# A top-k attention and MLP kernel on one core: TensorE's order written by hand, transposes in transpose mode, division on GpSimd, weights converted piece by piece

## The chip, the core and the metric

The kernel runs on one core of a Trainium2 chip. The metric is the device time of one execution in microseconds (us); the median of several executions counts. PE is TensorE, DVE VectorE, ACT ScalarE, POOL GpSimd, SP the engine whose queue issues the DMAs.

## The reference

```python
batch, n_heads, seq, head_dim = (8, 8, 576, 64)          # q, k, v
n_tokens, d_model, d_ff = (4608, 512, 2048)              # x, w_in, w_out
scores = scale * np.matmul(q, k.transpose(0, 1, 3, 2))
kth = np.partition(scores, -top_k, axis=-1)[..., -top_k:-top_k + 1]     # top_k = 32
scores = np.where(scores >= kth, scores, -1000000000.0)
scores = scores - np.max(scores, axis=-1, keepdims=True)
attn = np.exp(scores)
attn = attn / (np.sum(attn, axis=-1, keepdims=True) + 1e-09)
x = np.matmul(attn, v)                                    # then (B,H,S,D) -> (B*S, H*D)
h = x @ w_in
g = np.where(h >= 1, h, np.where(h <= -1, 0.0, (h + 1) ** 2 / 4.0))
out = g @ w_out
```

The weights arrive as 64-bit floats, two 32-bit words each, and the kernel turns them into 32-bit floats itself. All arithmetic is in 32-bit floats. A 32-bit matmul stands as two records of PE in the trace; a transpose in transpose mode as one.

## The kernel before

**Attention.** A row tile is 128 queries. A batch has 576 rows, so four whole tiles (t = 0 to 3) and 64 rows over; the leftover rows are done for two heads at a time (t = NT). One step is one tile for one pair of heads; there are 144 steps (`steps`, numbered m), four for each whole tile and two for each tail. A step has five stages, each a function. `scores` makes 128x576 scores per head in two halves of 288 columns (PSUM tiles `sp`, 64 contraction rows each) and ACT copies them to `s`. `top_k` finds the 32 largest of each row on DVE: four rounds of MAX8 and three of MATCH_REPLACE8, for each of the two heads (L192, L195). `weights` masks and exponentiates on ACT (L207, L209), adds up the sums `z`, takes 1/z on DVE (`z`, `rz`), and POOL writes `diag`, the identity times 1/z. `transpose_w` multiplies each 128-column block of the weights by `diag` (`pw`, L226), which transposes and divides at once, and does the last 64 columns apart (`pwt`, 64 output columns, L231). `values` multiplies the transposed weights by v (`po`) into `xT`.

**MLP.** It works on chunks of three row tiles (CT = 3, 384 columns). For each of 16 blocks f of the hidden width there are four matmuls over the contraction (`ph`, L277), then ACT makes `r` (L281), POOL squares it (L283), and DVE makes `g` (L284). For each tile, 16 matmuls over f then give `py` (L290), which ACT copies out to `y` and SP stores.

**Weight conversion.** There are 32 pieces of 128x512 (`weight_piece`): six DVE instructions and five POOL instructions each (L80 to L99), 16 pieces for `w_in` and then 16 for `w_out`. All are placed in the steps before the first chunk is ready; the first MLP matmul comes after the last piece.

**Order.** The loop over m issues `top_k(m)`, `scores(m+1)`, `weights(m-1)`, `transpose_w(m-2)`, half of this step's side work, `values(m-2)`, the other half. Side work is a generator (first the pieces, then one chunk's MLP at a time) that is advanced at an even rate. A scheduler of the tile framework then decides the order on each engine. PSUM has two banks for `sp` (tag `sc`), two for transposes (`tr`), two for `ph`, one each for `po` and `py`. All engines run their queues in order.

Of the kernel before, what the change touches and what calls it, by code (L numbers as in the profile page):

```python
# [1 line left out]

# [12 lines left out]
TOP_K = 32  # L15
# [4 lines left out]
def kernel(  # L20
# [26 lines left out]
    CT = 3  # L47
    CW = CT * P
    SCALE = float(D) ** -0.5
    FAR = 2.0 ** 80  # L50

# [12 lines left out]

    v_tails = []
    for i in range(2):
        v_tails.append(const.tile([P, H, D], F32, name=f"v_tail{i}"))
        nc.gpsimd.memset(v_tails[i], 0.0)
# [4 lines left out]
    def weight_piece(pool, dst, src):  # L73
# [9 lines left out]
        nc.vector.scalar_tensor_tensor(out=top, in0=lo, scalar=29, in1=top,  # L83
                                       op0=ALU.logical_shift_right, op1=ALU.bitwise_or)
# [15 lines left out]

    def weight_pieces(pool):
        for kk in range(NK):
            for c in range(0, DFF, WC):
                weight_piece(pool, w_in[:, kk, c:c + WC], moe_w_in[kk * P:(kk + 1) * P, c:c + WC])
                yield
        for f in range(NF):
            for c in range(0, DM, WC):
                weight_piece(pool, w_out[:, f, c:c + WC], moe_w_out[f * P:(f + 1) * P, c:c + WC])
                yield

# [5 lines left out]
    def load_values(b):  # L116
# [3 lines left out]
        for j in range(2):  # L120
            nc.sync.dma_start(out=v_tl[j * TL:(j + 1) * TL, j::2, :],
                              in_=v[b, j::2, SM:S, :].rearrange("h p d -> p h d"))
        return v_in, v_tl
# [10 lines left out]

    def keys_of(b):
# [5 lines left out]
        for hp in range(NHP):  # L141
# [3 lines left out]
            pt = ps.tile([P, NT, P], F32, name="pk", tag="tr", bufs=2)  # L145
            for c in range(NT):
                nc.tensor.transpose(pt[:, c, :], k_in[:, c].rearrange("p j d -> p (j d)"), ident)
            nc.scalar.copy(kT[:, hp, 0:SM], pt.rearrange("p c n -> p (c n)"))
            if hp == 0:
                pt = ps.tile([P, NHP, TL], F32, name="pkt", tag="tr", bufs=2)  # L150
# [3 lines left out]
                nc.scalar.copy(kT[:, :, SM:S], pt)  # L154
            yield dict(kT=kT, v=v_in, v_tl=v_tl)

    def queries_of(q_in, t):
        n = P if t < NT else TL
        qT = stage.tile([P, NHP, n], F32, name="qT" if t < NT else "qTt")
        pt = ps.tile([P, NHP, n], F32, name="pq", tag="tr", bufs=2)  # L160
# [258 lines left out]
```

## Time and profile before

| what | us |
|---|---|
| median of three runs | 2151.63 (2151.48 to 2151.65) |
| profiled execution, its own time | 2151.82 |
| its span, first to last instruction | 2150.0 |
| PE busy | 1923.7 (89%) |
| DVE busy | 1649.7 (77%) |
| ACT busy | 1008.3 (47%) |
| POOL busy | 527.1 (25%) |

The profile has four kinds of views used below. A table by stretches gives each engine's busy time between two moments. A timeline lists instructions in order of time, runs of the same kind merged. The chain that ended last follows the program back from its end, so each of its rows says how long the path stood on one thing. Groups by line give a mean time of one instruction. PE's matmuls overlap at their ends, so what a run of them costs is better read from one start to the next, as the chain has it, than from the mean of one.

### The profile page before, as it was taken

To read this page: it belongs to the slowest core of one execution; us is meant where nothing else is said; L and a number is where in the kernel's file an instruction comes from. 1 tells how busy PE (TensorE), PEld (TensorE's weight loads), DVE (VectorE), ACT (ScalarE), POOL (GpSimd) and SP (SyncE) were. 2 spreads that over 40 slices of the span, in tenths; PEclk is the share of its full clock that TensorE was granted. 3 is DMA by queue.
4 is the path that set the end of the run, shared out by engine and by line. 5 is a ranking of instruction groups with operands and counts; after the bars stand their busy time and mean duration, and the time that the engine had idled before them with its cause. 6 is when DMAs were issued, how large, how long until landed. Compare 5 with 4: busy or idle time off the path is not lost.

```text
span 2150.0 us, 29200 instructions
## 1 busy us (share of the span) xinstructions
PE 1923.7 (89%) x10560; PEld 1158.1 (54%) x10560; DVE 1649.7 (77%) x3568; ACT 1008.3 (47%) x2341; POOL 527.1 (25%) x809
## 2 busy tenths in 40 slices
PE   4333459999999999999999999999999999999999
PEld 2222336556556556556556556556556556555575
DVE  5888799978768779878768779878678779767530
ACT  3222245555445445545445446555445445454331
POOL 4889862102112112102112112102112112112021
PEclk9756779999999999999999999999999999999999
DMA  6222200100010000000010001000010000000000
GB/s 147 72 68 74 69 23 6 40 25 11 13 38 18 20 13 27 19 25 11 13 38 18 20 13 28 18 26 10 13 37 16 11 11 6 11 11 1 11 6 15
DMA packets 98193, 56.41 MB, mean 26 GB/s; under 512 B 81152, under 2 KB 89344, under 8 KB 98048
## 3 DMA queue, kind: packets, MB, share of 16 engines
q1 hardware_dynamic: 98048, 54.54, 9.3%
q8 instruction: 83, 1.36, 0.3%
q14 instruction: 62, 0.51, 0.1%
HBM read 45.09 MB, written 9.44 MB: 25 GB/s over the span
## 4 chain that ended last, share of the span: by engine, by line
PE 67%; DVE 19%; ACT 5%; POOL 5%; issue 3%; DMA 0%; SPq 0%; POOLq 0%; ACTq 0%; DVEq 0%
PE py L290 20%; PE ph L277 19%; PE pw L226 10%; PE sp L181 9%; DVE tops L192 8%; DVE rest L195 7%; PE po L247 5%; ACT s L183 2%; PE pwt L231 2%; POOL keep L94 1%; POOL low L98 1%; POOL low L97 1%; ACT s L207 1%; ACT s L209 1%; ACT r L281 1%
## 5 line engine op out<-in xcount | busy, mean ns | idle before, releaser
L192 DVE MAX8 tops<-rest 128x8 f32<-128x576 f32 x864 | 614.5, 748 | 0.1
L277 PE MATMUL ph<-xT,w_in 128*128 128x384 f32 (+2 forms) x1664 | 543.1, 472 | 2.3 <-DVE g L284 2.3
L290 PE MATMUL py<-w_out,g 128*128 128x512 f32 x1152 | 529.0, 603 | 0.0
L226 PE MATMUL pw<-diag,s 128*128 128x128 f32 x2304 | 345.3, 298 | 163.5 <-POOL diag L216 163.5
L226 PEld LDWEIGHTS pw<-diag,s 128*128 128x128 f32 x2304 | 296.9, 202 | 256.6 <-POOL diag L216 173.4
L195 DVE MATCH_REPLACE8 rest<-tops,rest 128x576 f32<-128x576 f32 x576 | 424.6, 743 | 0.0
L277 PEld LDWEIGHTS ph<-xT,w_in 128*128 128x128 f32 x1664 | 293.4, 190 | 183.9 <-issue 21.6
L207 ACT ACTIVATE s<-s,tops 128x576 f32<-128x576 f32 x288 | 217.1, 774 | 339.5 <-DVE tops L192 329.2
L290 PEld LDWEIGHTS py<-w_out,g 128*128 128x128 f32 x1152 | 208.0, 190 | 230.0 <-issue 224.4
L283 POOL TENSOR_TENSOR r<-r 128x384 f32<-128x384 f32 (+2 forms) x208 | 161.8, 778 | 638.1 <-ACT r L281 638.1
L192 DVE MAX8 tops<-s 128x8 f32<-128x576 f32 x288 | 208.0, 750 | 143.7 <-ACT s L183 143.5
L181 PE MATMUL sp<-kT,qT 64*128 64x288 f32 x1024 | 241.6, 464 | 39.3 <-ACT s L183 34.0
L183 ACT ACTIVATE s<-sp 128x288 f32<-128x288 f32 x576 | 210.7, 408 | 94.8 <-PE sp L181 89.5
L281 ACT ACTIVATE r<-ph,half 128x384 f32<-128x384 f32 (+2 forms) x208 | 115.2, 554 | 298.0 <-PE ph L277 297.6
L284 DVE SCALAR_TENSOR_TENSOR g<-ph,r 128x384 f32<-128x384 f32 (+2 forms) x208 | 109.2, 525 | 157.3 <-POOL r L283 156.0
L209 ACT ACTIVATE s<-s,nb 128x576 f32<-128x576 f32 x288 | 223.0, 775 | 1.5 <-POOL nb L204 0.4
L195 DVE MATCH_REPLACE8 rest<-tops,s 128x576 f32<-128x576 f32 x288 | 212.3, 743 | 0.0
L227 ACT COPY wT<-pw 128x512 f32<-128x512 f32 x288 | 167.2, 585 | 91.9 <-PE pw L226 90.8
L181 PEld LDWEIGHTS sp<-kT,qT 64*128 64x128 f32 x1024 | 115.7, 188 | 150.1 <-ACT s L183 79.8
L216 POOL TENSOR_SCALAR diag<-ident,rz 128x128 f32<-128x128 f32 x288 | 123.0, 440 | 288.2 <-PE pwt L231 134.0
L204 POOL TENSOR_TENSOR nb<-tops 128x2 f32<-128x2 f32 x144 | 29.9, 208 | 655.2 <-DVE tops L192 243.8
L247 PEld LDWEIGHTS po<-wT,v_in 128*64 128x64 f32 x2048 | 111.8, 138 | 71.5 <-issue 58.7
(55 smaller groups left out, 1180.3 us busy)
## 6 DMA issues: line engine op xcount, KB each, us to landing
q_in<-in_q_dram SPq DMA_DIRECT2D x32, 256.0 KB, 3.0
v_in<-in_v_dram SPq DMA_DIRECT2D x8, 1024.0 KB, 6.2
k_in<-in_k_dram SPq DMA_DIRECT2D x64, 128.0 KB, 2.8
raw<-in_moe_w_in_dram SPq DMA_DIRECT2D x16, 512.0 KB, 3.9
raw<-in_moe_w_out_dram SPq DMA_DIRECT2D x16, 512.0 KB, 3.6
out_dram<-y SPq DMA_DIRECT2D x32, 256.0 KB, 2.4
v_tail<-in_v_dram SPq DMA_DIRECT2D x16, 64.0 KB, 5.4
k_tl<-in_k_dram SPq DMA_DIRECT2D x8, 128.0 KB, 3.1
```

Source lines behind the costliest of these rows:

```text
L181: nc.tensor.matmul(o, qT[d, g, :], kT[d, g, keys], start=True, stop=True)
L183: nc.scalar.activation(s[:, i, keys], sp[i], AF.Copy, scale=SCALE)
L192: nc.vector.max(out=tops[:, i, r:r + 8], in_=src[:, i, :])
L195: nc.vector.match_replace(out=rest[:, i, :], in_to_replace=tops[:, i, r:r + 8], in_values=src[:, i, :], imm_value=LOWEST)
L207: nc.scalar.activation(s[:, i, :], s[:, i, :], AF.Prelu, bias=tops[:, i, TOP_K - 1:TOP_K], scale=-1.0, alpha=1.0 / FAR)
L209: nc.scalar.activation(s[:, i, :], s[:, i, :], AF.Exp, bias=nb[:, i:i + 1], scale=-FAR, accum_out=z[:, i:i + 1])
L226: nc.tensor.matmul(pt[:, c, :], w[:, i, c * P:(c + 1) * P], diag[:, i, :], start=True, stop=True)
L227: nc.scalar.copy(wT[:, i], pt)
L247: nc.tensor.matmul(po[j * D:(j + 1) * D], v_in[:, h, c, :] if c < NT else v_tl[:, h, :], wT[:, j, c, :] if c < NT else wTt, start=(c == 0) ...
L277: nc.tensor.matmul(ph, w_in[:, kk, f * P:(f + 1) * P], xT[:, kk, 0:cw], start=(kk == 0), stop=(kk == NK - 1))
L283: nc.gpsimd.tensor_tensor(out=r, in0=r, in1=r, op=ALU.mult)
L290: nc.tensor.matmul(py, gs[f][:, i * P:(i + 1) * P], w_out[:, f, :], start=(f == 0), stop=(f == NF - 1))
```

## The change

TensorE's order is now the order of the program text (`tc.manual_schedule` for PE alone); the other engines are still scheduled by the framework. Within a step the text has `values(m-2)`, `scores(m+1)`, MLP pieces, `transpose_w(m-1)`, the transposes of queries and keys, MLP pieces. Weights of step m are made in step m, not m+1.

- `transpose_w` uses transpose mode with the identity, nine blocks a step; the tails of both heads are one block of 128 columns. For that the scores of the second head are stored with the 64 tail columns first (`main`, `tail`, `pieces`), and a second copy of v's tails is loaded by four more DMAs a batch.
- The division is a POOL instruction on the 128x576 weights of each head, in place of `diag`.
- Mask and exponential have other constants and one more small POOL instruction (`nkth`).
- A weight piece has four DVE, two POOL and two ACT instructions. Three pieces are converted a step; `w_in` goes by column blocks, and MLP work may start as soon as its own pieces are there.
- MLP chunks have at most two tiles, the first two and the last two have one. The MLP is a list of pieces with a cost each, spread over the steps that are left.
- PSUM: four banks in one ring (tag `a`) for everything of attention, three for `ph`, one for `py`. `s` has three buffers in place of four.

```diff
-    CT = 3
+    CT = 2
...
+    PER_STEP = 3
...
-        nc.vector.scalar_tensor_tensor(out=top, in0=lo, scalar=29, in1=top,
-                                       op0=ALU.logical_shift_right, op1=ALU.bitwise_or)
 
         unit = pool.tile([P, WC], U32, name="unit")
         nc.vector.tensor_scalar(unit, top, 0xFF800000, None, ALU.bitwise_and)
-        rest = pool.tile([P, WC], U32, name="rest")
-        nc.vector.tensor_scalar(rest, lo, 0x1FFFFFFF, None, ALU.bitwise_and)
-
-        keep = pool.tile([P, WC], U32, name="keep")
-        nc.vector.tensor_scalar(keep, hi, 0x7FFFFFFF, None, ALU.bitwise_and)
-        keep = keep.bitcast(F32)
-        nc.gpsimd.tensor_scalar(keep, keep, 1.125 * 2.0 ** -15, None, ALU.is_ge)
         low = pool.tile([P, WC], F32, name="low")
-        nc.gpsimd.tensor_scalar(low, rest, 2.0 ** -26, 2.0 ** -26, ALU.mult, ALU.mult)
+        nc.scalar.activation(low, lo, AF.Copy, scale=2.0 ** -52)
         nc.gpsimd.tensor_tensor(out=low, in0=low, in1=unit.bitcast(F32), op=ALU.mult)
         nc.gpsimd.tensor_tensor(out=low, in0=low, in1=top.bitcast(F32), op=ALU.add)
-        nc.gpsimd.tensor_tensor(out=dst, in0=low, in1=keep, op=ALU.mult)
+
+        size = pool.tile([P, WC], F32, name="size")
+        nc.scalar.activation(size, hi.bitcast(F32), AF.Abs)
+        nc.vector.scalar_tensor_tensor(out=dst, in0=size, scalar=1.125 * 2.0 ** -15, in1=low,
+                                       op0=ALU.is_ge, op1=ALU.mult)
...
-        for kk in range(NK):
-            for c in range(0, DFF, WC):
+        for c in range(0, DFF, WC):
+            for kk in range(NK):
...
+        for hp in range(NHP):
+            g = hp % 2
+            nc.sync.dma_start(out=v_tl[1][g * TL:(g + 1) * TL, 2 * hp:2 * hp + 2, :],
+                              in_=v[b, 2 * hp:2 * hp + 2, SM:S, :].rearrange("h p d -> p h d"))
...
-        st["s"] = s = att.tile([P, 2, S], F32, name="s", bufs=4)
+        st["s"] = s = att.tile([P, 2, S], F32, name="s", bufs=3)
         for hf in range(2):
-            keys = slice(hf * SH, (hf + 1) * SH)
-            sp = [ps.tile([P, SH], F32, name="sp", tag="sc", bufs=2) for _ in range(2)]
...
+            sp = [ps.tile([P, SH], F32, name="sp", tag="a", bufs=4) for _ in range(2)]
+            c0, c1 = hf * SH, (hf + 1) * SH
             for i in range(2):
                 for j in ([i] if t < NT else [0, 1]):
                     d = slice(j * D, (j + 1) * D)
                     g = hp if t < NT else hp + i
                     o = sp[i] if t < NT else sp[i][j * TL:(j + 1) * TL]
-                    nc.tensor.matmul(o, qT[d, g, :], kT[d, g, keys], start=True, stop=True)
+                    for a0, a1, k0 in pieces(i, j, c0, c1):
+                        nc.tensor.matmul(o[:, a0 - c0:a1 - c0], qT[d, g, :], kT[d, g, k0:k0 + a1 - a0],
+                                         start=True, stop=True)
...
+    def mask(x, nkth):
+        nc.scalar.activation(x, x, AF.Prelu, bias=nkth, alpha=FAR)
+
     def weights(st):
         s, tops = st["s"], st["tops"]
+        nkth = att.tile([P, 2], F32, name="nkth")
+        nc.gpsimd.tensor_scalar(nkth, tops[:, :, TOP_K - 1], -1.0, 1.0, ALU.mult, ALU.mult)
         nb = att.tile([P, 2], F32, name="nb")
         nc.gpsimd.tensor_tensor(out=nb, in0=tops[:, :, TOP_K - 1], in1=tops[:, :, 0], op=ALU.subtract)
         z = att.tile([P, 2], F32, name="z")
         for i in range(2):
-            nc.scalar.activation(s[:, i, :], s[:, i, :], AF.Prelu, bias=tops[:, i, TOP_K - 1:TOP_K], scale=-1.0,
-                                 alpha=1.0 / FAR)
-            nc.scalar.activation(s[:, i, :], s[:, i, :], AF.Exp, bias=nb[:, i:i + 1], scale=-FAR,
-                                 accum_out=z[:, i:i + 1])
+            mask(s[:, i, :], nkth[:, i:i + 1])
+            nc.scalar.activation(s[:, i, :], s[:, i, :], AF.Exp, bias=nb[:, i:i + 1], accum_out=z[:, i:i + 1])
         rz = att.tile([P, 2], F32, name="rz")
         nc.vector.tensor_scalar(z, z, 1e-9, None, ALU.add)
         nc.vector.reciprocal(rz, z)
-        st["diag"] = diag = att.tile([P, 2, P], F32, name="diag")
         for i in range(2):
-            nc.gpsimd.tensor_scalar(diag[:, i, :], ident, rz[:, i:i + 1], 1.0, ALU.mult, ALU.mult)
+            nc.gpsimd.tensor_scalar(s[:, i, :], s[:, i, :], rz[:, i:i + 1], 1.0, ALU.mult, ALU.mult)
 
 
     def transpose_w(st):
-        t, w, diag = st["t"], st["s"], st["diag"]
+        w = st["s"]
         st["wT"] = wT = att.tile([P, 2, NT, P], F32, name="wT")
         st["wTt"] = wTt = att.tile([P, P], F32, name="wTt")
         for i in range(2):
-            pt = ps.tile([P, NT, P], F32, name="pw", tag="tr", bufs=2)
+            pt = ps.tile([P, NT, P], F32, name="pw", tag="a", bufs=4)
             for c in range(NT):
-                nc.tensor.matmul(pt[:, c, :], w[:, i, c * P:(c + 1) * P], diag[:, i, :], start=True, stop=True)
+                nc.tensor.transpose(pt[:, c, :], w[:, i, main(i)][:, c * P:(c + 1) * P], ident)
             nc.scalar.copy(wT[:, i], pt)
-        pt = ps.tile([P, P], F32, name="pwt", tag="po")
-        for i in range(2):
-            if t < NT:
-                nc.tensor.matmul(pt[i * TL:(i + 1) * TL], w[:, i, SM:S], diag[:, i, :], start=True, stop=True)
-            else:
-                for j in range(2):
-                    nc.tensor.matmul(pt[j * TL:(j + 1) * TL, i * TL:(i + 1) * TL], w[:, i, SM:S],
-                                     diag[:, i, j * TL:(j + 1) * TL], start=True, stop=True)
+        pt = ps.tile([P, P], F32, name="pwt", tag="a", bufs=4)
+        nc.tensor.transpose(pt, w.rearrange("p i n -> p (i n)")[:, SM:SM + P], ident)
...
+        got = []
+        for f in range(NF):
+            got.append((NK * len(tiles), NK * (f * P // WC + 1), partial(hidden, f)))
+        for i in range(len(tiles)):
+            for f in range(0, NF, 2):
+                got.append((2 * DM // P, n_pieces - NF + f + 2, partial(final, i, f, f + 2)))
+        return got
...
-            chunks += [a[0:3], a[3:4] + c[0:2], c[2:4] + [tl]]
+            chunks += ([a[0:1], a[1:2]] if b == 0 else [a[0:2]]) + [a[2:4], c[0:2], c[2:4], [tl]]
...
-            chunks += [a[0:3], a[3:4] + [tl] + c[0:1], c[1:3], c[3:4]]
+            chunks += [a[0:2], a[2:4], [tl], c[0:2], c[2:3], c[3:4]]
...
     def advance(amount):
-        nonlocal due
+        nonlocal spent, due
         due += amount
-        while due >= 1.0:
-            due -= 1.0
-            next(side, None)
-
+        while pending and pending[0][1] <= converted and due >= pending[0][0]:
+            cost, _, work = pending.popleft()
+            due -= cost
+            spent += cost
+            work()
+        due = min(due, 8.0)
+
+    order = tc.manual_schedule(engines={mybir.EngineType.PE})
+    order.__enter__()
...
     for m in range(n + 2):
+        if 2 <= m:
+            values(state[m - 2])
+            state[m - 2] = None
+            for ch in [c for c in range(len(chunks)) if ready[c] == m - 2]:
+                pending.extend(mlp(xTs[ch], chunks[ch], mlp_pool))
+        share = (total - spent) / (n + 2 - m)
         if m < n:
             top_k(state[m])
         if m + 1 < n:
             begin(m + 1)
+        if m < n:
+            weights(state[m])
+        convert(PER_STEP / 2)
+        advance(share / 2)
         if 1 <= m <= n:
-            weights(state[m - 1])
-        if 2 <= m:
-            transpose_w(state[m - 2])
-        advance(rate / 2)
+            transpose_w(state[m - 1])
+        queries(m + 2)
```

The order on three engines, in the middle of the program. On PE the place is some steps in which a chunk's hidden blocks are made. `sp` are scores, `pw` and `pwt` the transposes of the weights, `po` the values, `ph` and `py` the two MLP matmuls, `pq` and `pk` transposes of queries and keys. Before:

```order
L277 MATMUL ph<-xT,w_in 128x384 x4
L162 MATMUL pq<-ident,q_in 128x128 x4
L226 MATMUL pw<-diag,s 128x128 x4
L181 MATMUL sp<-kT,qT 128x288 x2
L226 MATMUL pw<-diag,s 128x128 x3
L181 MATMUL sp<-kT,qT 128x288 x2
L226 MATMUL pw<-diag,s 128x128
L231 MATMUL pwt<-diag,s 64x128 x2
L277 MATMUL ph<-xT,w_in 128x384 x4
L247 MATMUL po<-wT,v_in 64x128 x8
L247 MATMUL po<-wTt,v_tail_81 64x128 x2
L290 MATMUL py<-w_out,g 128x512 x4
```

PE after the change, again one step and a bit:

```order
L269 MATMUL po<-wT,v_in 64x128 x8
L269 MATMUL po<-wTt,v_tail_83 64x128 x2
L206 MATMUL sp<-kT,qT 128x288 x4
L300 MATMUL ph<-xT,w_in 128x256 x8
L254 MATMUL pw<-ident,s 128x128 x8
L257 MATMUL pwt<-ident,s 128x128
L300 MATMUL ph<-xT,w_in 128x256 x12
L269 MATMUL po<-wT,v_in 64x128 x8
L269 MATMUL po<-wTt,v_tail_83 64x128 x2
L206 MATMUL sp<-kT,qT 128x288 x4
```

Scores now follow the values without a full-width matmul between them and are no longer broken up; transposes stand next to MLP pieces. Counted over the whole order, PE goes from one of the three kinds (128x64 tiles: `po` and the old `pwt`; 64-row tiles: `sp`; full width: the rest) to another 1043 times before and 431 times after.

On DVE the place is the end of one `top_k` and the start of the next. Before:

```order
L195 MATCH_REPLACE rest<-tops,rest 128x576 x2
L192 MAX tops<-rest 128x8 x2
L212 TENSOR_SCALAR z<-z 128x2
L284 SCALAR_TENSOR_TENSOR g<-ph,r 128x384
L213 RECIPROCAL rz<-z 128x2
L192 MAX tops<-s 128x8 x2
L195 MATCH_REPLACE rest<-tops,s 128x576 x2
```

DVE after:

```order
L221 MATCH_REPLACE rest<-tops,rest 128x576 x2
L218 MAX tops<-rest 128x8 x2
L307 SCALAR_TENSOR_TENSOR g<-ph,r 128x256 x2
L218 MAX tops<-s 128x8 x2
L221 MATCH_REPLACE rest<-tops,s 128x576 x2
L241 TENSOR_SCALAR z<-z 128x2
L218 MAX tops<-rest 128x8
L242 RECIPROCAL rz<-z 128x2
L307 SCALAR_TENSOR_TENSOR g<-ph,r 128x256 x2
```

Before, the `z` behind a `top_k` was that of the step before; now it is that of the same step, a few instructions into the next `top_k`.

On POOL the place is the queue around the division. Before:

```order
L283 TENSOR_TENSOR r<-r 128x384 x2
L204 TENSOR_TENSOR nb<-tops 128x2
L216 TENSOR_SCALAR diag<-ident,rz 128x128 x2
L283 TENSOR_TENSOR r<-r 128x384 x2
L204 TENSOR_TENSOR nb<-tops 128x2
```

POOL after:

```order
L306 TENSOR_TENSOR r<-r 128x256 x2
L244 TENSOR_SCALAR s<-s,rz 128x576 x2
L306 TENSOR_TENSOR r<-r 128x256 x3
L233 TENSOR_SCALAR nkth<-tops 128x2
L235 TENSOR_TENSOR nb<-tops 128x2
L244 TENSOR_SCALAR s<-s,rz 128x576 x2
```

The two divisions of 576 columns stand where the two `diag` of 128 columns stood, with squares of `r` queued right behind them.

## Rows read from the trace of the kernel before

**Rows 1.** Table by stretches: us, busy time and count per engine, granted PE clock, DMA.
```profile
0.00:358.00 358.00, 168.04 (x962) 115.49 (x962) 291.43 (x601) 121.17 (x277) 256.92 (x230) 0.76 0.25 69
358.00:2150.00 1792.00, 1755.66 (x9600) 1042.64 (x9599) 1358.30 (x2968) 887.10 (x2064) 270.18 (x579) 1.00 0.07 18
```
**Rows 2.** Chain that ended last, around 1111 us: start, us it stood there, what.
```profile
1111.13 1.98 PE pw L226 x16
1113.12 0.37 PE pwt L231 x4
...
1116.26 1.24 PE po L247 x20
1117.50 2.78 PE ph L277 x8
1120.28 0.44 PE pq L162 x4
...
1121.61 0.69 PE sp L181 x4
...
1122.94 1.00 PE sp L181 x3
```
**Rows 3.** The same chain, a chunk of two tiles (256 columns).
```profile
2053.14 3.65 PE ph L277 x16
```
**Rows 4.** Timeline of DVE around one `top_k`: start, us, engine, line, operation.
```profile
1002.05 0.68 DVE L212 TENSOR_SCALAR z<-z 128x2 f32<-128x2 f32 x1
...
1004.15 1.42 DVE L192 MAX8 tops<-s 128x8 f32<-128x576 f32 x2 [0.78 <-ACT s L183]
...
1006.94 1.41 DVE L192 MAX8 tops<-rest 128x8 f32<-128x576 f32 x2
...
1013.73 1.41 DVE L192 MAX8 tops<-rest 128x8 f32<-128x576 f32 x2
1015.06 0.15 DVE L212 TENSOR_SCALAR z<-z 128x2 f32<-128x2 f32 x1
```
**Rows 5.** Groups by line: count, busy us, mean ns of one, idle before.
```profile
L81 DVE SCALAR_TENSOR_TENSOR top<-raw,top 128x512 uint32<-128x512 uint32 x32 | 29.5, 921 | 0.0
L98 POOL TENSOR_TENSOR low<-low,top 128x512 f32<-128x512 f32 x32 | 40.6, 1268 | 2.5
L94 POOL TENSOR_SCALAR keep<-keep 128x512 f32<-128x512 f32 x32 | 60.5, 1892 | 7.3 <-DVE keep L92 7.3
L96 POOL TENSOR_SCALAR low<-rest 128x512 f32<-128x512 uint32 x32 | 26.5, 827 | 17.8 <-DVE rest L89 16.2
L204 POOL TENSOR_TENSOR nb<-tops 128x2 f32<-128x2 f32 x144 | 29.9, 208 | 655.2 <-DVE tops L192 243.8 <-DVE z L212 223.3 <-DVE rz L213 87.1
L284 DVE SCALAR_TENSOR_TENSOR g<-ph,r 128x256 f32<-128x256 f32 x16 | 6.8, 423 | 23.6 <-POOL r L283 23.6
```
**Rows 6.** Timeline around 210 us, the stretch of the weight conversion.
```profile
208.84 1.44 ACT L207 ACTIVATE s<-s,tops 128x576 f32<-128x576 f32 x2 [13.47 <-DVE tops L192]
...
209.44 0.42 DVE L80 TENSOR_SCALAR top<-raw 128x512 uint32<-128x512 uint32 x1
...
210.11 2.28 POOL L216 TENSOR_SCALAR diag<-ident,rz 128x128 f32<-128x128 f32 x2 [0.20 <-DVE rz L213]
...
211.61 0.19 ACT L209 ACTIVATION_READ_ACCUMULATOR s<-s,nb 128x1 f32 x1
```
**Rows 7.** The chain at the start.
```profile
2.96 0.61 SPq L121
...
27.71 1.32 DVE tops L192 x2
```
**Rows 8.** The chain at the end.
```profile
2134.89 1.78 PE ph L277 x16
...
2138.43 7.74 PE py L290 x18
...
2146.24 0.59 ACT y L295
```

More of the change, by code (lines that the diff above doesn't have):

```diff
@@ L1 @@
+from collections import deque
 from contextlib import ExitStack
+from functools import partial
 import concourse.bass as bass
@@ L66 @@
     for i in range(2):
-        v_tails.append(const.tile([P, H, D], F32, name=f"v_tail{i}"))
-        nc.gpsimd.memset(v_tails[i], 0.0)
+        v_tails.append([const.tile([P, H, D], F32, name=f"v_tail{i}{x}") for x in range(2)])
+        for x in v_tails[i]:
+            nc.gpsimd.memset(x, 0.0)
     WC = 512
@@ L132, in load_queries, with main, tail, pieces @@
         return q_in
+    def main(i):
+        return slice(0, SM) if i == 0 else slice(TL, S)
+    def tail(i):
+        return slice(SM, S) if i == 0 else slice(0, TL)
+    def pieces(i, j, c0, c1):
+        if i == j:
+            return [(c0, c1, c0)]
+        cuts = [(0, TL, SM), (TL, S, 0)] if i else [(0, SM, TL), (SM, S, 0)]
+        return [(max(a, c0), min(b, c1), o + max(a, c0) - a) for a, b, o in cuts if max(a, c0) < min(b, c1)]
     def keys_of(b):
@@ L153, in keys_of @@
                                         ident[0:TL, 0:TL])
-                nc.scalar.copy(kT[:, :, SM:S], pt)
+                for j in range(2):
+                    d = slice(j * D, (j + 1) * D)
+                    nc.scalar.copy(kT[d, :, tail(j)], pt[d])
             yield dict(kT=kT, v=v_in, v_tl=v_tl)
@@ L273, in mlp, with hidden @@
         gs = []
-        for f in range(NF):
-            ph = ps.tile([P, CW], F32, name="ph", tag="ph", bufs=2)[:, 0:cw]
+        def hidden(f):
+            ph = ps.tile([P, CW], F32, name="ph", tag="ph", bufs=3)[:, 0:cw]
             for kk in range(NK):
@@ L318, with convert @@
     ready = [max(m for m in range(n) if steps[m][3] == ch) for ch in range(len(chunks))]
-    units = [NF + len(tiles) * (NF // 4) for tiles in chunks]
-    n_pieces = NK * DFF // WC + NF * DM // WC
-    cvt = tc.tile_pool(name="cvt", bufs=1)
-    cvt_pool = cvt.__enter__()
-    mlp_pool = None
-    side, left, rate, due = weight_pieces(cvt_pool), n_pieces, n_pieces / (ready[0] + 1), 0.0
+    mlp_pool = ctx.enter_context(tc.tile_pool(name="mlp", bufs=1))
+    pieces_left = weight_pieces(mlp_pool)
+    pending = deque()
+    total, spent = sum(len(tiles) for tiles in chunks) * (NK * NF + NF * DM // P), 0
+    converted, owed, due = 0, 0.0, 0.0
+    def convert(amount):
+        nonlocal converted, owed
+        owed += amount
+        while owed >= 1.0 and converted < n_pieces:
+            owed -= 1.0
+            converted += 1
+            next(pieces_left)
     def advance(amount):
-        nonlocal due
+        nonlocal spent, due
         due += amount
-        while due >= 1.0:
-            due -= 1.0
-            next(side, None)
+        while pending and pending[0][1] <= converted and due >= pending[0][0]:
[6 more added lines that the diff above has]
+    order.__enter__()
     keys, xTs = {}, {}
@@ L346, with queries @@
     state = []
+    def queries(m):
+        if m < n and steps[m][0:2] not in qTs:
+            r = steps[m][0:2]
+            qTs[r] = queries_of(q_ins[r], r[1])
+            fetch(rounds.index(r) + 2)
     def begin(m):
         b, t, hp, ch, col = steps[m]
-        if (b, t) not in qTs:
-            qTs[b, t] = queries_of(q_ins[b, t], t)
-            fetch(rounds.index((b, t)) + 2)
         if ch not in xTs:
```

64 lines of the change are left out of this document (29 added, 35 removed).

## The prediction

> **What bounds the kernel now.** I read the table by stretches first. The program has two parts [rows 1]. In the first 358 us the weights are converted: DVE is busy 291 us of them and POOL 257, PE only 168, at a granted clock of 0.76 on average. In the other 1792 us PE is busy 1755.66 us (98%) at full clock, DVE 1358 (76%), POOL 270 (15%). So POOL and DVE set the first part and PE the second. The chain says what PE's time goes into [rows 2]: one step's transposes take 1.98 us in 16 records and its tail block 0.37, values 1.24, scores 0.69 where both halves find a bank and 1.00 where one waits. Sixteen records at 0.11 make 1.78, so about 0.2 us of the 1.98 is the change from one kind of tile to another; the 3.65 us of sixteen hidden records of 256 columns [rows 3] hold the same 0.2, which leaves 0.216 for a record. An output record takes 7.74 / 18 = 0.43 [rows 8].
>
> DVE's own price of a step comes from its timeline [rows 4]. From 1004.15 to 1006.94 it does two MAX8 and two MATCH_REPLACE8, 2.79 us; from 1013.73 to 1015.06 the last two MAX8, 1.33. A `top_k` is three of the first and one of the second, 9.70 us. `z` and `rz`, two instructions of 0.15 and a little between, make it 10.05 a step, or 1447 us for 144 steps. That does not change, and it becomes the floor.
>
> **PE after the change.** A transpose in transpose mode is one record: four `pq` take 0.44 us [rows 2], 0.11 each. Nine are 0.98 in place of 1.98 + 0.37, which saves 1.37 us a step, 197 us in all. Scores with four banks take 2 x 0.69 in place of 0.69 + 1.00, 0.3 less. The changes of tile kind fall from 1043 to 431; 612 at 0.2 would be 122 us, part of which is in the two savings already. Without MLP a step is then values 1.24, scores 1.38, transposes 0.98, changes 0.1: 3.7 us. The MLP itself hardly gets cheaper: a hidden block of two tiles is 8 x 0.216 = 1.73, two output matmuls 4 x 0.43 = 1.72.
>
> The Trainium skill speaks against the transposes: "TensorE: Matmul & The Clock Gate", part 4 (PE-mode transpose), gives about 275 ns for one in a kernel. The rows above have 0.11 us, so I use that; by the page's figure nine would be 2.5 us, and my sum would grow as in the rival below.
>
> **DVE, POOL and ACT.** Steps get `g` in smaller pieces: 352 in place of 208, 0.42 us for 256 columns [rows 5], some 0.38 on average with those of 128. Division: no row shows it. Below, one-input POOL work on 512 columns takes 0.83 (L96), above, 1.89 (L94) [rows 5]; for 576 columns that is 0.93 to 2.1. I take 1.0, nearest to L96, which also multiplies by constants; two make 2 us a step, and POOL's total stays far below a step. It lies beside other work as long as the transposes of a step come one step later. What can show is contention: a `z` took 0.68 instead of 0.15 [rows 4], and two `diag` took 2.28 us while DVE converted weights [rows 6]. POOL will be busy some third of the time, so 0.53 us in a third of the steps is 25 us on DVE; it lies inside the range and not in the sum. The Trainium skill has a rule here that speaks against the change: "GPSIMD Engine Reference", 8. Key points, says that GpSimd shares its SBUF interfaces with VectorE, and that VectorE is about twice as fast at such work. The 0.68 us agrees with the sharing. If a `z` were held in every step, 0.53 x 144 = 76 us would be added; a division moved to DVE would lengthen the engine that is the floor, so I keep it on POOL in the sum.
>
> **The wait that is added.** `z` of a step now stands in the next `top_k`, usually behind two MAX8 and two MATCH_REPLACE8, 2.79 us. What it waits for is longer: one small POOL instruction of 0.21 [rows 5], then mask and exponential of both heads on ACT, 208.84 to 211.80, 2.96 us [rows 6], and the hops between, 3.4 in all. Behind `z` on DVE stands the rest of that `top_k`, for which the next mask on ACT and so the next transposes wait. I walked DVE's written order and counted what stands between the last MAX8 and `z` at these prices: in steps 13 to 142 the shortfall from 3.4 us adds up to 119 us. It costs only in the steps that DVE sets.
>
> **The sum.** Start to the first MAX8: 27.7 us [rows 7]. Four DMAs of v's tails go ahead of the keys on SP, 4 x 0.65 from the 0.61 of one [rows 7], but DVE then did conversion work before its first MAX8 that may move: 29.
>
> Steps 0 to 12, with 32 pieces: 13 x 10.05 = 131. A piece on DVE is two instructions of 0.42 [rows 6], one of 0.92 (L81 [rows 5]), and a last one that no row shows; between 0.42 and 0.92, taken as 0.75 because it reads two tensors: 2.5, or 80 in all. POOL's two instructions of 1.27 [rows 5] stand between the third and the last of them, and DVE's order has some 1.4 us of `top_k` there, so 1.1 is waited: 35. With 28 small `g`, 8: together 254 us. PE has slack there, as it had before at its lower clock [rows 1].
>
> Steps 13 to 142, walking both orders and taking the longer engine in each step: 14 steps without MLP are DVE's 10.05, 141 (PE has 3.7 us there, or 7.4 at 1.2 GHz, the lower of its two levels; the mean of 0.76 in the first part lies between them [rows 1]). In 33 steps with 116 `g` DVE is longer, 33 x 10.05 + 116 x 0.38 = 376. In 75 steps PE is longer, 908: 3.7 each and 8.4 of MLP, mostly five pieces of 1.73. In the last 8 steps the pieces pile up to 12 us, 125. That is 1550. To it come the waits for `z` in the 47 steps of DVE, 33, and the 2% that PE was not busy while it set the time before, 30. Against it stands that the queues run ahead of each other: `s` has three buffers and `ph` three banks. Summed over three steps at a time, the longer engine makes 37 less. 1576.
>
> The end: values, transposes and the MLP of one tile, 8 x 1.78 + 32 x 0.43 = 28 [rows 8], with 1.2 before it, and from the last `py` to the end of the span 2150.0 - 2146.24 = 3.8: 33.
>
> 29 + 254 + 1576 + 33 = 1892 us of span. The profiled execution was 1.8 longer than its span (2151.82 against 2150.0) and 0.2 above the median, so I forecast **1894 us**, 12% less.
>
> **Rivals.** (1) The two fixed orders even out fully and PE alone sets the steps, 1420 us for steps 13 to 142 and 2% more: 29 + 254 + 1450 + 33 + 2 = 1768; with DVE's sum and all its waits instead, 1410 + 119 = 1529, it is 1847. For it: PE ran at 98% before with a DVE that was 76% busy. Against: each engine now needs nearly the whole step, 10.9 and 10.8 us.
>
> (2) The small waits do not hide in each other: all of `z`, no evening out, 2% more. 1894 + 86 + 37 + 30 = 2047. For it: in order queues do add up waits; before 16 `g` of one form DVE stood 23.6 us for POOL, 1.5 each [rows 5], with time to spare then.
>
> (3) Slower: the squares of `r` are queued right behind the division on POOL. If DVE reaches a `g` before its square is through, it stands still for the division, which itself waits for `rz` on DVE. At 2.1 us a head that is 4.3 us in each of the 77 steps with hidden blocks, 331 us: 2225. It turns the sign from 3.3 us a step on. Against it: by the written orders a `g` stands some 3 us or more of DVE work later than its square can be ready, so PE would wait for a bank first.
>
> (4) The change does not do what it says, the transposes get no cheaper: at 0.275 us nine cost 1.5 more; in the 83 steps of PE that is 124, in the 33 others 0.7 each, 23: 2041.
>
> **Chances and range.** Forecast, both engines by turns, 1847 to 1940: 0.48. Rival 1, 1768 to 1847: 0.22. Rival 2, 1940 to 2060: 0.22. Rival 3: 0.05. Rival 4: 0.03. The range of 8 in 10 takes the forecast whole, rival 1 from 1790 up and rival 2 to 1990: 1790 to 1990. The division at its high end or the pieces at 0.42 or 0.92 move it by 10 to 30 and lie inside. Faster by over 0.2%, which is what a measurement of this kernel can tell from no change: 0.94; the same 0.01; slower 0.05.
>
> **What would show it.** In the new profile: `pw` near 0.11 us a record and nine a step; DVE busy above 85% after 250 us; its idle time mostly before `z` and before MAX8 on new scores, not before `g`; the conversion over by 285 us; PE below 95%. It is wrong if idle time before `g` passes 250 us, if the division takes over 2.5 us, or if the step in the middle is over 13 us or under 11.

## The result and the profile after

The changed kernel takes 2019.48 us (median of four runs, 2017.94 to 2021.12), beside 2151.56 for the kernel before: a ratio of 0.9387, 95% interval 0.937 to 0.9403. It is faster, as forecast, but by 6% and not by 12%: the forecast was 1894, and its range ended at 1990. The profiled execution took 2018.67 us, with a span of 2016.9.

Four views show where the time lies. First the page, with its busy line and the shares of the chain of waits by engine:

```profile
PE 1717.6 (85%) x10128; PEld 1175.6 (58%) x10128; DVE 1608.3 (80%) x3648; ACT 1075.0 (53%) x2589; POOL 537.6 (27%) x1003
...
DVE 53%; PE 19%; ACT 12%; POOL 10%; issue 6%; DMA 1%; SPq 0%; POOLq 0%; DVEq 0%; ACTq 0%
```

The table by stretches, cut at the first MAX8 of step 13 (278.5 us) and of step 143, the last (1956.3):

```profile
core 0: us, PE busy (x) PEld busy (x) DVE busy (x) ACT busy (x) POOL busy (x), PEclk, DMA share, GB/s
0.00:278.50 278.50, 130.90 (x756) 95.95 (x757) 206.06 (x440) 133.95 (x293) 126.06 (x153) 0.73 0.31 89
278.50:1956.30 1677.80, 1530.13 (x9037) 1040.61 (x9035) 1385.88 (x3162) 923.37 (x2253) 400.13 (x822) 0.96 0.07 19
1956.30:2016.90 60.60, 56.53 (x340) 39.08 (x338) 16.40 (x46) 17.65 (x45) 11.37 (x28) 0.99 0.03 9
```

The middle, steps 13 to 142, takes 12.9 us a step, with PE busy 91% of it and DVE 83%. Neither engine is full, where before PE was 98% busy [rows 1], so something ties them together. The waits of the changed kernel (engine, line and tile, what it waited for, us in total, times, longest) name it:

```profile
ACT s L228 <- POOL nkth L233: 315.2, 126, 7.3
...
DVE tops L218 <- ACT s L209: 202.7, 81, 7.4
...
DVE g L307 <- POOL r L306: 71.3, 92, 15.6
PE pw L254 <- POOL s L244: 64.1, 9, 13.8
PE sp L206 <- ACT xT L282: 57.6, 35, 5.1
...
DVE z L241 <- ACT s L239: 48.2, 17, 5.1
```

DVE stands still for 203 us before the first MAX8 of a step, for the copies of the scores, and PE for 58 us in the middle of the scores, for the copy of `xT`. The prediction had looked for DVE's idle time before `z` as well; that is only 48 us. One step shows how it happens, in the timeline of all engines (start, us, instruction, and in brackets the idle time ahead of it with what ended it); step 42's `top_k` ends here and step 43's begins:

```profile
632.27 1.41 DVE L218 MAX8 tops<-rest 128x8 f32<-128x576 f32 x2
...
633.47 0.39 PE L269 MATMUL po<-wTt,v_tail 128*64 128x128 f32 x4
...
633.79 1.23 PE L206 MATMUL sp<-kT,qT 64*128 64x288 f32 x6
633.85 0.19 POOL L233 TENSOR_SCALAR nkth<-tops 128x2 f32<-128x2 f32 x1 [5.36 <-DVE tops L218]
...
634.07 1.44 ACT L228 ACTIVATE s<-s,nkth 128x576 f32<-128x576 f32 x2 [4.15 <-POOL nkth L233]
635.42 0.24 ACT L282 COPY xT<-po 128x128 f32<-128x128 f32 x1
635.56 0.41 ACT L209 ACTIVATE s<-sp 128x288 f32<-128x288 f32 x1
...
635.71 0.75 PE L206 MATMUL sp<-kT,qT 64*128 64x288 f32 x2 [0.69 <-ACT xT L282]
...
636.62 1.00 ACT L209 ACTIVATE s<-sp 128x288 f32<-128x288 f32 x3
637.43 1.42 DVE L218 MAX8 tops<-s 128x8 f32<-128x576 f32 x2 [3.74 <-ACT s L209]
```

`po` is ready at 633.86, but ACT copies it to `xT` only at 635.42: in ACT's order both masks of step 42 stand ahead of it, they wait for `nkth`, and that waits for the end of `top_k`. `po` and the four score tiles are five tiles in a ring of four banks, so the last two score matmuls wait for that copy. They then take 0.75 us by themselves, where six before them took 1.23. Behind the masks stand the copies of the scores too, with an exponential among them. So `top_k`, `nkth`, masks, `xT`, last scores and copies run one after the other: 9.86 us of `top_k` from 623.82 to 633.68 and 3.74 of idle time, 13.6 us a step, for which PE's own work would be 12.3 (3.7 and ten output matmuls at 0.86).

### The profile page after: what moved, and what is told of

Read it like the earlier page. It is cut to its first block, busy times and chain, and to the rows that moved or that the text cites. A ratio compares the mean times of both kernels' runs of the same rounds, so it can differ in the third digit from the quotient of the medians.

```text
span 2016.9 us, 29329 instructions
## 1 busy us (share of the span) xinstructions
PE 1717.6 (85%) x10128; PEld 1175.6 (58%) x10128; DVE 1608.3 (80%) x3648; ACT 1075.0 (53%) x2589; POOL 537.6 (27%) x1003
## 4 chain that ended last, share of the span: by engine, by line
DVE 53%; PE 19%; ACT 12%; POOL 10%; issue 6%; DMA 1%; SPq 0%; POOLq 0%; DVEq 0%; ACTq 0%
DVE tops L218 27%; DVE rest L221 20%; PE py L315 9%; PE ph L300 4%; ACT s L228 4%; ACT s L239 3%; DVE g L307 3%; POOL s L244 3%; ACT s L209 2%; POOL r L306 2%; PE sp L206 2%; POOL low L93 2%; PE po L269 2%; POOL low L94 2%; PE pw L254 2%
## 5 line engine op out<-in xcount | busy, mean ns | idle before, releaser
L300 PE MATMUL ph<-xT,w_in 128*128 128x256 f32 (+1 forms) x2816 | 560.4, 355 | 72.0 <-DVE g L307 71.8
L300 PEld LDWEIGHTS ph<-xT,w_in 128*128 128x128 f32 x2816 | 466.2, 197 | 158.0 <-DVE g L307 87.9
L228 ACT ACTIVATE s<-s,nkth 128x576 f32<-128x576 f32 x288 | 214.4, 772 | 315.4 <-POOL nkth L233 315.2
L244 POOL TENSOR_SCALAR s<-s,rz 128x576 f32<-128x576 f32 x288 | 217.6, 768 | 382.0 <-DVE rz L242 243.1
L306 POOL TENSOR_TENSOR r<-r 128x256 f32<-128x256 f32 (+1 forms) x352 | 187.8, 540 | 423.6 <-ACT r L304 418.4
L206 PE MATMUL sp<-kT,qT 64*128 64x288 f32 x1024 | 196.8, 452 | 60.2 <-ACT xT L282 51.2
L304 ACT ACTIVATE r<-ph,half 128x256 f32<-128x256 f32 (+1 forms) x352 | 148.2, 433 | 172.8 <-PE ph L300 141.3
L254 PE MATMUL pw<-ident,s 128*128 128x128 f32 x1152 | 163.5, 288 | 68.8 <-POOL s L244 64.1
L254 PEld LDWEIGHTS pw<-ident,s 128*128 128x128 f32 x1152 | 142.9, 149 | 119.5 <-POOL s L244 72.6
L307 DVE SCALAR_TENSOR_TENSOR g<-ph,r 128x256 f32<-128x256 f32 (+1 forms) x352 | 128.6, 368 | 76.4 <-POOL r L306 71.3
```

The lines of the kernel that those rows point to most:

```text
L206: nc.tensor.matmul(o[:, a0 - c0:a1 - c0], qT[d, g, :], kT[d, g, k0:k0 + a1 - a0], start=True, stop=True)
L228: nc.scalar.activation(x, x, AF.Prelu, bias=nkth, alpha=FAR)
L244: nc.gpsimd.tensor_scalar(s[:, i, :], s[:, i, :], rz[:, i:i + 1], 1.0, ALU.mult, ALU.mult)
L254: nc.tensor.transpose(pt[:, c, :], w[:, i, main(i)][:, c * P:(c + 1) * P], ident)
L300: nc.tensor.matmul(ph, w_in[:, kk, f * P:(f + 1) * P], xT[:, kk, 0:cw], start=(kk == 0), stop=(kk == NK - 1))
L306: nc.gpsimd.tensor_tensor(out=r, in0=r, in1=r, op=ALU.mult)
```

## The experiments

Every change below is made to the changed kernel. Four theories were tried on the 125 us by which the span is over its forecast: (A) ACT's order, as just told; (B) lumps, that PE is simply full in steps with five pieces of the MLP, and DVE's wait only shows it; (C) the ring of banks alone; (D) the granted clock, 0.96 in the middle, which the forecast had named for the steps without MLP and priced at nothing.

**mask_after: one mask behind the scores' copies.**

```
-                nc.scalar.activation(s[:, i, c0:c1], sp[i], ...)
+                st["copied"] = nc.scalar.activation(s[:, i, c0:c1], sp[i], ...).ins
...
-            mask(s[:, i, :], nkth[:, i:i + 1])
+            with tc.issue_after(after["copied"]) if after and i == 0 else nullcontext():
+                mask(s[:, i, :], nkth[:, i:i + 1])
```

`after` is the state of the next step; the guard itself binds instructions on ACT alone. The rest of the scheduler's orders on ACT, DVE and POOL changes with it; PE's stays.

> Edit: on ACT the first mask of a step is ordered behind the last copy of the next step's scores; nothing else. Theory A (ACT's order: in steps with output matmuls the mask of the step stands ahead of the copies of xT and of the next scores, so DVE waits through top_k, mask, xT, last scores, copy, 13.6 us a step): DVE's idle time before MAX8 on new scores falls from 203 us to under 110, PE's wait for xT from 58 to under 20, time 1930 to 1975. Theory B (the planner's lumps: PE is full in those steps, and DVE's wait only shows it): DVE's idle time moves elsewhere, time 2000 to 2030. A later mask could also make z late; then idle time before z grows from 48 us by what is won, and the time stays.

Measured 2007.39 us, 12 less: within B's range, but not as a test of A. PE's wait for `xT` is still 55.8 us: only head 0 was held, and ACT now takes the mask of head 1 first. DVE's wait for scores did not fall but rose, while the one before `z` went from 48 to 9:

```profile
DVE tops L218 <- ACT s L209: 234.0, 86, 7.0
...
DVE z L242 <- ACT s L240: 8.9, 6, 3.3
```

Half a test; the next one holds both.

**masks_after: both masks** (`if after and i == 0` becomes `if after`).

> Edit: as mask_after, with the masks of both heads behind the last copy of the next scores; in mask_after ACT simply took the mask of the other head first (one mask still ran ahead of xT in most steps), so its 12 us are half a test. Theory A (ACT's order): PE's wait for xT falls from 58 us to under 20, steps with 20 output records from 13.6 us to about 12.3, time 1950 to 1990. Theory B (lumps alone): 1998 to 2025, the idle time only changes its place, most likely to z, whose masks come later.

Measured 1907.52 us (1905.91 to 1908.32), 112 less than the changed kernel and beyond what either theory gave. The same place in this kernel's timeline:

```profile
615.48 1.41 DVE L218 MAX8 tops<-rest 128x8 f32<-128x576 f32 x2
616.05 1.09 PE L270 MATMUL po<-wT,v_in 128*64 128x128 f32 x16
616.98 0.39 PE L270 MATMUL po<-wTt,v_tail 128*64 128x128 f32 x4
...
617.30 1.24 PE L206 MATMUL sp<-kT,qT 64*128 64x288 f32 x8
617.41 0.27 ACT L283 COPY xT<-po 128x128 f32<-128x128 f32 x1 [3.99 <-PE po L270]
618.08 1.32 ACT L209 ACTIVATE s<-sp 128x288 f32<-128x288 f32 x4 [0.40 <-PE sp L206]
...
619.20 1.42 DVE L218 MAX8 tops<-s 128x8 f32<-128x576 f32 x2 [2.31 <-ACT s L209]
619.26 1.46 ACT L228 ACTIVATE s<-s,nkth 128x576 f32<-128x576 f32 x2
```

`xT` is copied as soon as `po` is ready, the eight score matmuls run as one group of 1.24 us, and the masks come last. The step takes 12.2 us in place of 13.6, which is PE's own work. Its waits say the same, and so does its chain by engine:

```profile
DVE tops L218 <- ACT s L209: 134.3, 63, 6.7
...
PE sp L206 <- ACT xT L283: 9.3, 7, 2.2
...
DVE z L242 <- ACT s L240: 6.6, 5, 3.1
```

```profile
PE 62%; DVE 20%; ACT 8%; POOL 7%; issue 3%; DMA 1%; SPq 0%; POOLq 0%; ACTq 0%; DVEq 0%
```

PE's wait for `xT` falls from 58 us to 9, DVE waits a third less for scores, and PE holds 62% of the chain where it held 19%. DVE is busy for 1608 us in both kernels, so what it waits less is what the kernel gains: 68 us before MAX8 on new scores and 42 before `z`. What the masks' later place was feared to do, hold `z` back, does not show, and one reason lies on DVE. Counted over its order in steps 13 to 142, 13 `z` of the changed kernel stand ahead of the next step's first MAX8, and 40 us of the wait before `z` fall on these. In masks_after none does, and 104 of 130 stand behind six instructions of the next `top_k`. So the 68 us go with the copies that the masks no longer hold up. The 42 come with a `z` that the scheduler put later, and no run holds that apart.

**x_first: masks behind the copy of `xT` only.** The same guard, on the copy in `values` of the same pass of the loop:

```
+            ran["xT"] = nc.scalar.copy(xT[:, hp, col:col + P], po).ins
...
+            with tc.issue_after(ran["xT"]) if ran else nullcontext():
+                mask(s[:, i, :], nkth[:, i:i + 1])
```

> Edit: ACT's masks of a step are ordered behind the copy of xT only (which gives po's bank to the last pair of score matmuls), not behind the copies of the scores. If the link that costs is the bank (xT's copy late, last scores alone on PE), most of masks_after's 112 us come back: 1905 to 1940, and PE's wait for xT falls under 20 us. If it is the copies of the scores themselves that stand behind the masks, PE's wait goes and DVE's idle time before MAX8 on new scores stays: 1970 to 2015.

Measured 1975.8 us. Its waits:

```profile
DVE tops L218 <- ACT s L209: 215.0, 83, 6.7
...
DVE z L244 <- ACT s L242: 9.5, 5, 5.9
...
PE sp L206 <- ACT xT L285: 7.8, 5, 3.0
```

PE's wait falls from 58 to 8 us and 44 us come off; the other 68 of the 112 come only when the copies of the scores go ahead of the masks as well. DVE's wait for scores is not shorter than in the changed kernel (215 against 203); what it waits less is 39 us before `z`, which again no longer stands ahead of the first MAX8, and 13 before `g`. How much of the 44 us is the bank's is therefore not shown. So the larger link is the one that the prediction did not see at all: new scores that lie ready in a bank while ACT waits with a mask for the `top_k` that DVE is in.

**ring5: five banks for `a`, two for `ph`.**

```
-tag="a", bufs=4   -tag="ph", bufs=3
+tag="a", bufs=5   +tag="ph", bufs=2
```

> Edit: five PSUM banks for po, scores and transposes, two for the hidden blocks. Theory C (five tiles in four banks: po and four score tiles): PE's wait for xT falls from 58 us to under 10 and the four score tiles keep running two at a time: 40 to 60 us less, 1960 to 1980. Theory A: scores get done but their copies still stand behind the mask, so DVE's idle time before MAX8 on new scores stays above 150 us and under 25 us is won, 1995 to 2020; with only two banks for hidden blocks, PE may wait for g and lose 10 to 20 of it.

Each tile with one of the tags has the new number. Measured 2064.03 us, 45 slower, which neither theory had. PE no longer waits for `xT`, but the third bank of the hidden blocks was worth more:

```profile
PE ph L300 <- DVE g L307: 173.2, 101, 25.2
```

That was 71.8 us in the changed kernel. DVE's wait for scores stays, at 207 us, as A had it. A bank for C has to come from somewhere, and eight are all in use here. The run tells little on C itself; x_first does that without a bank.

**warm: idle transposes to hold the clock.**

```
+        if not pending and converted >= n_pieces:
+            pd = ps.tile([P, P], F32, name="warm", tag="ph", bufs=3)
+            for _ in range(16):
+                nc.tensor.transpose(pd, ident, ident)
         due = min(due, 8.0)
```

> Edit: in half steps where no MLP piece is pending, 16 idle transposes of the identity run on PE, their result unread. Theory D (the granted clock: 0.96 on average from 400 us on, half rate in stretches that follow PE's idle time, which makes some 30 to 40 us): granted clock 0.98 or more in the middle, 20 to 40 us less, 1980 to 2000. Theories A and B: within 8 us of 2019, since steps without MLP are set by DVE and the heavy steps by their content.

Measured 2057.96 us, 38 slower, which no theory had. From 303 to 349 us, two steps without MLP and the two behind them, the clock does rise; first the changed kernel, then this one:

```profile
303.00:349.00 46.00, 37.95 (x273) 29.46 (x272) 42.48 (x97) 28.48 (x69) 11.44 (x23) 0.89 0.08 20
```

```profile
303.00:349.00 46.00, 41.97 (x358) 34.70 (x356) 42.67 (x97) 27.43 (x67) 10.21 (x21) 1.00 0.08 20
```

But the first step without MLP grows from 9.79 to 12.79 us: PE comes late for the next scores, and DVE waits 2.9 us for them (234 us in all, 203 before). **masks_warm** puts the same lines into masks_after, to take that link away.

> Edit: masks_after with warm's 16 idle transposes in half steps where no MLP piece is pending. In warm they took PE's slack away just where ACT's order then made DVE wait. If that coupling was why it lost, and the granted clock is worth something, 1880 to 1903 here. If the idle transposes simply make PE late for the next scores, 1915 to 1945 again.

Measured 1919.2 us, 12 over masks_after, although the mean clock is 0.954 and not 0.938. PE's slack in those steps was worth more than what the clock gave back, if it gave anything: no run separates the two, and a clock held in some other way was not tried. D stays open.

**plan_even and taut: other shares of the MLP.** In plan_even a step's share is what is pending divided by the steps until the next chunk is ready. In taut it is the largest constant rate that never runs dry before a chunk comes:

```
-        share = (total - spent) / (n + 2 - m)
+        ends = [(sum(len(t) for x, t in enumerate(chunks) if ready[x] + 2 < e), e)
+                for e in [r + 2 for r in ready if r + 2 > m] + [n + 2]]
+        share = max(0, min((128 * tiles - spent) / (e - m) for tiles, e in ends if tiles))
```

> Edit: the MLP's share of a step is what is pending divided by the steps until the next chunk is ready, in place of what is left of the whole program. Theory B (lumps): steps without MLP and steps with five pieces both go, a middle step takes 11.3 to 12 us in place of 12.9, and the last step is left with one chunk in place of two: time 1850 to 1930. Theory A (ACT's order): steps with output matmuls still take 13 us or more, and the time is 1970 to 2015.

> Edit: the MLP's share of a step is the largest constant rate that never runs out of work before a chunk is ready, so that most steps get four pieces (6.9 us of PE beside 3.7) and neither empty steps nor lumps stay, which plan_even still had at three places (two steps of 31 us each). Theory B: a middle step of 11 to 11.8 us, time 1800 to 1870. Theory A would still find output steps at 13 us or more, time above 1900.

Measured 1968.18 and 1958.18 us, 51 and 61 less. plan_even made lumps of its own, at three places two steps of 31 to 33 us, where a chunk of one tile comes two steps after another. taut has none, and 101 of its 130 middle steps carry four pieces; it still waits 176 us for scores, so B alone does not give the time either. The uneven plan does cost, though: it is the plan that the forecast had counted, step by step. **taut_masks** is taut with both masks moved:

> Edit: taut and masks_after together. Theory A (ACT's order costs on its own, whatever the load): 20 to 50 us under taut. Theory B (the order costs only where PE is behind DVE, and with even steps it is not): within 15 us of taut, or over it, since masks behind a late copy hold z back.

Measured 1835.78 us: 122 under taut, where A had 20 to 50, and no less than on the uneven plan. DVE's wait for scores falls from 176 to 84 us. A costs by itself, on either plan; even steps do not heal it. Beside masks_after the even plan is worth 72 us.

**diag: transposes back to matmuls.** `weights` makes `diag` on GpSimd in place of dividing `s`, and `transpose_w` multiplies by it (20 records a step in place of nine, 16 for `pw` and four for `pwt`; the 18 below is a miscount, while its 1.37 us holds all 20):

```
-                nc.tensor.transpose(pt[:, c, :], w[:, i, main(i)][:, c * P:(c + 1) * P], ident)
+                nc.tensor.matmul(pt[:, c, :], w[:, i, main(i)][:, c * P:(c + 1) * P], diag[:, i, :],
+                                 start=True, stop=True)
```

> Edit: the transposes go back to matmuls with diag(rz), and GpSimd makes two 128x128 diagonals in place of dividing 128x576 twice; order and all else as in the changed kernel. By the prediction's prices PE has 1.37 us more a step (18 records in place of nine), which counts in the some 85 steps that PE sets: 2100 to 2150. If the transposes are covered by DVE in most steps, 2020 to 2060.

Measured 2098.83 us, 79 more, just under the first range. The true transposes with their division are worth 79 us of the change, as much as 58 steps at 1.37 us.

**old_conv: the old weight pieces** (the body of `weight_piece` from the kernel before).

> Edit: the weight conversion of the kernel before (more instructions on DVE and five on GpSimd a piece), in the changed kernel's order by piece. By the rows of before, a piece costs DVE about 1 us more and GpSimd 2.5 to 3 us more; 32 pieces: 30 to 80 us later at step 13 and the rest as it was, 2050 to 2100. If the conversion is covered by the scores' work, within 15 of 2019.

Measured 2074.78 us, 55 more. Of the 61.5 us between the profiled spans, 57 lie ahead of step 13, which begins at 335.8 us and not at 278.5; what follows takes 1742.6 us beside 1738.4. The first stretch of this kernel:

```profile
0.00:335.80 335.80, 135.61 (x749) 97.75 (x750) 250.59 (x505) 94.31 (x225) 266.72 (x248) 0.67 0.26 74
```

DVE is busy 44.5 us more and POOL 141, which is 1.4 and 4.4 us a piece.

**auto_pe: PE's order left to the scheduler** (`manual_schedule` taken out).

> Edit: PE's order is left to the scheduler, all else as in the changed kernel. The scheduler mixes kinds of tiles more, so changes of the kind come more often at some 0.1 to 0.2 us each: 2030 to 2080 if the written order is worth what its saved changes are. If ACT's order sets the time, PE's order hardly counts, or its freedom to run past a blocked score pair even helps: 1980 to 2025.

Measured 1992.15 us, 27 less than with the written order. **auto_masks** does the same to masks_after, **taut_masks_auto** to taut_masks:

> Edit: masks_after with PE's order left to the scheduler. If the written order on PE is itself a part of the loss (auto_pe was 27 us under the changed kernel), these 27 come off again: 1875 to 1890. If auto_pe only happened to give ACT a better order, PE's order no longer counts once the masks are fixed: 1895 to 1920; the few more changes of tile kind then cost 10 or nothing.

> Edit: taut_masks with PE's order left to the scheduler. With even steps PE has some 10.6 us of work beside DVE's 9.8 to 11.6, so a few more changes of tile kind lie in its slack: 1830 to 1845 if the written order is worth nothing, over 1850 if its saved changes count, under 1825 if its fixed order blocks.

Measured 1871.97 us, 36 under masks_after, and 1822.61, 13 under taut_masks. So leaving PE's order to the scheduler wins on every plan, most on the uneven one. The orders of ACT, DVE and POOL change with it, so that not all of it need lie on PE. And the written order saves few changes of tile kind: counted over PE's records, auto_pe has 500 and the changed kernel 431. One thing that the scheduler does shows in the hidden blocks' share of the table by stretches, over DVE's steps 14 to 16, in which PE passes the two steps that the plan leaves without MLP, first of the changed kernel, then of auto_pe (PE's records in brackets):

```profile
291.30:322.50 31.20, 0.00 (x0) 0.00 (x0) 0.00 (x0) 0.00 (x0) 0.95 0.05 15
```

```profile
282.80:313.40 30.60, 4.69 (x18) 3.17 (x18) 0.00 (x0) 0.00 (x0) 0.94 0.05 16
```

It starts the next blocks there with the parts of `xT` that exist already. That this is the whole 27 us was not tested.

**taut_masks_end: the last four chunks of one tile each**, on top of taut_masks (`c[0:2]` becomes `c[0:1], c[1:2]`).

> Edit: taut_masks, with the last four chunks of one tile each, so that less of the MLP is left for the last ten steps (8.6 us a step in place of 10.3). Gain of some 1.5 us in each of the last eight steps, less a little for more instructions on DVE: 1820 to 1835. Within 5 us of 1836 if the end is set by the last chunk alone.

Measured 1854.9 us, 19 slower than taut_masks, a miss: the smaller tail of the plan did not pay for twice as many hidden blocks of those two tiles. Where they cost was not followed up.

The fastest is taut_masks_auto: 1822.61 us (1822.35 to 1827.25), 0.8476 of the kernel before, interval 0.8463 to 0.8489.

## Why the prediction was off

The span of 2016.9 us against the sum of 1892, by the sum's own parts:

- **Start and steps 0 to 12**: 283 forecast, 278.5 measured. The first MAX8 comes at 23.6 us (29 forecast), the rest takes 254.9 (254). DVE's instructions of a piece take 510, 678, 439 and some 720 ns, 2.35 us in place of 2.5, and it waits 42.6 us for POOL in place of 35. The last piece is done at 253 us. Right.
- **Steps 13 to 142**: 1576 forecast, 1677.8 measured, 102 over. With only the masks' order changed, masks_after needs 1566.5 here (its stretch is shown below). This is the step that failed. "Scores with four banks take 2 x 0.69" left out that `po` uses a bank of the same ring, and "the queues run ahead of each other", which took 37 us off, left out ACT: the sum had walked PE's and DVE's orders and never ACT's, where a mask that waits for DVE stands ahead of copies that DVE waits for. Moving the masks behind the copy of `xT` alone takes off 44 us (x_first), behind the copies of the scores as well another 68 (masks_after), just what DVE then waits less for scores. The term for `z` was near in size, 33 against 44 measured here. The agreement of 1566.5 with 1576 is partly luck: the sum held 33 us for `z`, which masks_after does not have, and held nothing for the written order, whose removal takes 28 us more off the middle (1538.0 in auto_masks). The span also ends near the sum, 1905.3 against 1892, with an end that took 30 us more.
- **The end**: 33 forecast, 60.6 measured from the first MAX8 of step 143. Step 143 itself was forgotten: 13 and 130 steps make 143 of 144. Its `top_k` ends at 1967.7. From there PE is busy 17.0 of 17.2 us, until the last tile's hidden blocks start at 1984.9: it still has work of the tile before. The last eight steps of the middle, which the sum had heavy throughout, took 112.7 us on DVE (125 forecast), three of them 9.8 to 10.7 and five 15.9 to 17.5. The last tile then takes 28.2 us, as forecast.

The middle of masks_after, in the columns of the table above:

```profile
275.50:1842.00 1566.50, 1479.30 (x9045) 1027.85 (x9044) 1386.09 (x3161) 923.36 (x2250) 398.29 (x820) 0.97 0.08 21
```

The terms themselves held. Step prices, by groups of instructions (columns as on the page):

```profile
L254 PE MATMUL pw<-ident,s 128*128 128x128 f32 x1152 | 163.5, 288 | 68.8 <-POOL s L244 64.1
...
L244 POOL TENSOR_SCALAR s<-s,rz 128x576 f32<-128x576 f32 x288 | 217.6, 768 | 382.0 <-DVE rz L242 243.1
```

Eight `pw` take 1.04 us in the timeline at 628.04 us, 0.11 each and nine a step, as forecast:

```profile
628.04 1.04 PE L254 MATMUL pw<-ident,s 128*128 128x128 f32 x8
```

The 288 ns of the group's row is the length of one record, and records overlap. The Trainium skill's 275 ns for a PE transpose ("TensorE: Matmul & The Clock Gate", part 4) is near that length; as a price in a stream it would have given rival 4's 2041, close to the measured time for a reason that is not there. The division takes 0.77 us, under its lower bound of 0.93. `top_k` with `z` and `rz` takes 9.8 us where nothing holds it (steps 16 and 26), 10.05 forecast.

The rivals: the time fell in the range of rival 2 (1940 to 2060, chance 0.22), and "small waits that do not hide in each other" is nearer than the forecast. But its price was put on `z` (48 us measured, 17 times), and the wait that counts is another. Rival 3 did not come: idle time before `g` is 71 us, far below 250. Of the signs, `pw`, the end of the conversion, PE below 95% and a middle step between 11 and 13 us were right. DVE at 83% was not above 85%, and the idle time lies before MAX8 on new scores, named second, hardly before `z`. The rule from "GPSIMD Engine Reference", 8. Key points, of the Trainium skill, that GpSimd shares SBUF interfaces with VectorE, costs little here: `z` is 0.16 us in the middle of its 144 instances, and at most 0.63. The trace agrees with the sharing and shows its form. The 12 `z` over 0.3 us, and no others, begin while POOL is in a multiply of two tensors, and each ends 24 to 28 ns after it:

```profile
54.41 1.27 POOL L93 TENSOR_TENSOR low<-low,unit 128x512 f32<-128x512 f32 x1 [2.19 <-ACT s L239]
...
55.09 0.62 DVE L241 TENSOR_SCALAR z<-z 128x2 f32<-128x2 f32 x1
```

No `z` begins during a division, but six L85 of the weight pieces do, and they take 0.89 us where most others take some 0.41. MAX8 and MATCH_REPLACE8, 251 of which begin during a division, take 0.74 to 0.76 as ever.

## What to carry to other kernels

When an order is written out for one engine, walk the order of every in-order engine around it, the one that only copies above all: an instruction that waits for engine X must not stand ahead of a copy for which X waits. Count all tiles that share a ring of banks in the same stretch, not those of one function. And before writing an order by hand, measure the scheduler's with the same parts: here the hand's order saved 69 changes of tile kind beside the scheduler's, and was 27 us slower.

## What the runs showed of the hardware

- Score matmuls of the two heads, on different rows of the array, run side by side: eight take 1.24 us in a row, where one after another would be some 1.9 (an estimate from 0.216 us for 256 columns [rows 3]). Split by a wait they take 1.23 for six and 0.75 for two, so the wait of 0.69 us cost its own length and some 0.7 us more.
- The granted clock is 0.89 on average from 303 to 349 us: 1.00 and 0.83 in the two steps without MLP (302.9 to 312.7 and 312.7 to 322.5 us, PE busy 7.5 of 9.8 us in each), and 0.82 in a step after them in which PE is busy all the time (334.5 to 348.0). Idle transposes, which raised it to 1.00 there, made the kernel slower, with or without ACT's order in the way.
- VectorE's tensor_scalar instructions that begin while GpSimd is in a multiply take longer (`z` 0.36 to 0.63 us in place of 0.16, L85 0.89 in place of 0.41); MAX8 and MATCH_REPLACE8 do not.
- GpSimd multiplies 128x576 by a per-row value in 0.77 us, less than the 0.83 us that it took for 128x512 in the kernel before (L96 [rows 5], which reads whole numbers).
